# A pinned order for the head of a fused attention and two-layer network kernel, with a score bank pair for each of the first four units and eight products with zeros

## The chip, the cores and the metric

The kernel runs on one core of a Trainium2 chip. The metric is the device time of one execution in microseconds (us); less is better. TensorE (PE in the rows; PEld is its weight load) multiplies, VectorE (DVE) and ScalarE (ACT) work on elements, SyncE (SP) issues the DMAs. Each engine executes its own instructions strictly in the order in which they stand in its queue, and an instruction waits at the head of its queue until what it needs is there.

## The reference, cut to what matters

Sliding-window attention with global tokens gives x (2304 rows of 512), then two feed-forward layers follow, each with 2048 hidden columns. The change touches the attention of the first tokens and the start of the first layer.

```python
s_l = concat([q_l @ k_g.T, where(|i - j| <= 32, q_l @ k_l.T, -1e9)]) / 8
out_l = softmax(s_l) @ concat([v_g, v_l])        # 4 batches, 8 heads, 512 rows, 64 columns
x = out.transpose(0, 2, 1, 3).reshape(2304, 512)
h = x @ w_in
g = maximum(h, 0) + alpha * minimum(h, 0)        # PReLU
x = g @ w_out
h = x @ w2_in
x = (h * clip(h + 3, 0, 6) / 6) @ w2_out
```

## The kernel before

**Attention units.** The local attention is cut into 32 units: one batch, one half of the 512 rows, one pair of heads. A unit loads q and k (`qk_t`) and v (`v_t`), computes 32 small score products (`s_ps`, L208), takes the masked maxima on VectorE (L226, four of them with their read-outs), four exponentials on ScalarE (L230), a sum and a reciprocal on VectorE (L232, L234; operations on 128x4), four transposes of the probabilities on TensorE (`pt_ps`, L241), a copy of them out of PSUM (`pt`, L243, ScalarE), the products with v (`o_ps`, L254) and a scaling on VectorE (`xo`, L260). Units are worked off in pairs, and both units of a pair write their scores into one pair of PSUM banks.

**First layer.** Products in float32 are made of three products of parts: every operand is split into a high part (a rounding copy on ScalarE) and a low part (a subtraction on VectorE). The outputs of four units (one per pair of heads) make 256 rows of x: they are transposed (`xt_ps`, L426) and split into `xt` (L409 high, L410 low). The weights arrive as 64-bit floats and are converted by hand, in halves of 128x512 (`Weights.convert`): ScalarE makes the low words usable (`raw`, L110), VectorE scales the high words (`z`, L113), merges both by two bit operations (L121, L123), and then the half is split (`wt`, L132 high on ScalarE, L133 low on VectorE). Each of the 16 column blocks j has two halves, one for the product into the hidden layer and one for the product out of it. A hidden step s is a group of 12 products (`h_ps`, L459), the PReLU (`t`, L469 on ScalarE and L471 on VectorE) and the split of its result (`g`, L477 high, L478 low); two steps later come the 12 products out of the layer (`y_ps`, L490).

**Block 0.** The first block of 512 rows begins with its first 256 rows, which four units give (units 0 to 3): steps 0 to 3 work on these with columns j = 0 to 3. Units 4 to 7 give the second 256 rows; steps 4 to 7 repeat j = 0 to 3 on them, and from step 8 on the products are 128x512 wide, over both halves. This document calls the `xt` of units 4 to 7 the second half of x.

**What sets the order.** A scheduler orders each engine's queue by its own estimate of times. An instruction passed through `here(...)` (keep_in_program_order) keeps its place in the order of the code relative to the others so marked. Before, the marks stand on the first two steps of a weight conversion and on `c1_sb`; the rest of the head is the scheduler's. `while not ready(blocks[0][:1])` drives the attention generator until units 0 to 3 are done, with a weight half converted at its steps 3, 4 and 5 (`CONVERT`). `bank()` hands out PSUM banks, in the head in turn from two pools of four.

**Head and rest.** Eight products of zeros (`warm_ps`, L87) stand at the very start of TensorE's queue.

## Time and profile before

| what | value |
|---|---|
| time, median of 3 runs | 825.03 us (823.32 to 825.47) |
| time of the profiled execution | 823.27 us |
| its span, first to last instruction | 821.5 us |
| mean granted clock of TensorE over the span | 0.993 of 2.4 GHz |
| busy TensorE / VectorE / ScalarE | 809.2 / 596.6 / 423.3 us |
| TensorE without a gap | from about 50 us to the end stage |

A row of the timeline gives the start of an instruction (or of a run of equal ones), its length, engine, line of the kernel, tile written <- tiles read, shape and count; in brackets the time that the engine sat idle before it and what released it. Rows of equal instructions overlap by some 0.1 us, since the end of one is recorded after the next has begun; the distance from one start to the next is what an instruction costs its queue.

### The profile page before, as it was taken

The page shows a single profiled execution, that of the slowest core. Times are in us where ns is not written, and L with a number is a line of the kernel's source. Part 1 is how long each engine was busy: PE and PEld are TensorE (multiplying, and loading weights), DVE is VectorE, ACT ScalarE, POOL GpSimd, SP SyncE. Part 2 cuts the span into 40 slices and gives each one's busy share as a digit, 9 for nine tenths or more (in the row PEclk, how much of TensorE's full clock was granted, in tenths as well). Part 3 has the DMA queues.
Part 4 walks back from the last instruction along what each step waited for, and adds up shares of the span by engine and source line. Part 5 has one row for each costly group of instructions (what it writes and reads, how often), then busy time and mean ns, then how long its engine had stood idle before and what let it go on. Part 6 is the DMA issues. An engine that isn't in the chain of part 4 may idle for free.

```text
span 821.5 us, 17564 instructions
## 1 busy us (share of the span) xinstructions
PE 809.2 (99%) x6980; PEld 714.1 (87%) x6980; DVE 596.6 (73%) x1247; ACT 423.3 (52%) x886; POOL 0.2 (0%) x4
## 2 busy tenths in 40 slices
PE   7999999999999999999999999999999999999997
PEld 4788888888888887888999988889999888899997
DVE  4998997477888776756878847778867576678443
ACT  5887996445656664544545524434553343333431
POOL 0000000000000000000000000000000000000000
PEclk8899999999999999999999999999999999999999
DMA  9985674347879767788495575576686656655663
GB/s 334 354 276 193 244 251 149 107 175 261 280 252 305 246 236 250 276 282 284 159 335 174 167 257 180 183 225 207 185 268 212 201 186 204 180 181 159 208 182 108
DMA packets 78002, 183.09 MB, mean 223 GB/s; under 512 B 6752, under 2 KB 28512, under 8 KB 77920
## 3 DMA queue, kind: packets, MB, share of 16 engines
q1 hardware_dynamic: 77728, 181.83, 66.9%
q8 instruction: 55, 0.90, 0.4%
q14 instruction: 27, 0.22, 0.1%
q10 hardware_dynamic: 192, 0.13, 0.1%
HBM read 139.47 MB, written 42.47 MB: 221 GB/s over the span
## 4 chain that ended last, share of the span: by engine, by line
PE 93%; DVE 2%; ACT 2%; DMA 1%; SPq 1%; issue 0%; DVEq 0%; ACTq 0%
PE y_ps L490 23%; PE h_ps L459 22%; PE o_ps L904 20%; PE k_ps L816 19%; PE s_ps L208 2%; PE o_ps L254 2%; PE yr_ps L789 1%; PE hr_ps L768 1%; DMA raw<-in_w 1%; PE pt_ps L241 1%; ACT p L230 1%; PE go_ps L391 1%; PE xt_ps L426 1%; PE gs_ps L346 1%; DVE z L121 1%
## 5 line engine op out<-in xcount | busy, mean ns | idle before, releaser
L490 PE MATMUL y_ps<-g,wt 128*128 128x512 f32 (+2 forms) x1008 | 205.4, 353 | 0.2 <-ACT g L477 0.2
L459 PE MATMUL h_ps<-xt,wt 128*128 128x512 f32 (+2 forms) x1008 | 203.2, 352 | 1.9 <-DVE xt L410 1.6
L459 PEld LDWEIGHTS h_ps<-xt,wt 128*128 128x128 f32 x1008 | 169.2, 190 | 24.0 <-DVE xt L410 2.0
L490 PEld LDWEIGHTS y_ps<-g,wt 128*128 128x128 f32 x1008 | 166.7, 189 | 22.2 <-issue 0.8
L904 PE MATMUL o_ps<-ws,gh 128*128 128x256 f32 x896 | 160.9, 283 | 0.1
L816 PE MATMUL k_ps<-bt,ws 128*128 128x512 f32 x672 | 157.2, 390 | 0.0
L816 PEld LDWEIGHTS k_ps<-bt,ws 128*128 128x128 f32 x672 | 124.6, 188 | 24.9
L904 PEld LDWEIGHTS o_ps<-ws,gh 128*128 128x128 f32 x896 | 138.8, 192 | 0.6 <-issue 0.3
L904 PE MATMUL o_ps<-ws,gl 128*128 128x256 f32 x448 | 124.2, 283 | 0.0
L830 DVE TENSOR_TENSOR gl<-far,gh 128x1024 fp32r<-128x1024 f32 x56 | 68.5, 1223 | 42.3 <-ACT gh L829 42.3
L829 ACT CAST gh<-far 128x1024 fp32r<-128x1024 f32 x56 | 58.7, 1048 | 74.4 <-PE o_ps L904 70.6
L904 PEld LDWEIGHTS o_ps<-ws,gl 128*128 128x128 f32 x448 | 84.9, 192 | 0.0
L471 DVE SCALAR_TENSOR_TENSOR t<-t,c_sb,h_ps 128x512 f32<-128x512 f32 (+2 forms) x84 | 53.0, 641 | 30.0 <-ACT t L469 29.6
L750 ACT ACTIVATE t<-far,half_sb 128x512 f32<-128x512 f32 x48 | 34.8, 724 | 77.1 <-DVE far L746 77.1
L469 ACT ACTIVATE t<-h_ps 128x512 f32<-128x512 f32 (+2 forms) x76 | 41.5, 550 | 51.0 <-PE h_ps L459 49.0
L478 DVE TENSOR_TENSOR g<-t,g 128x512 fp32r<-128x512 f32 (+2 forms) x76 | 48.0, 632 | 20.8 <-ACT g L477 18.4
L477 ACT CAST g<-t 128x512 fp32r<-128x512 f32 (+2 forms) x76 | 43.8, 576 | 34.7 <-DVE t L471 33.4
L230 ACT ACTIVATE p<-p,st 128x128 f32<-128x128 f32 x128 | 49.7, 389 | 11.6 <-DVE st L226 11.6
L121 DVE SCALAR_TENSOR_TENSOR z<-z,raw 128x512 uint32<-128x512 uint32 x64 | 43.6, 689 | 9.1 <-ACT z L116 4.6
L110 ACT ACTIVATE raw<-raw,quarter_sb 128x512 uint32<-128x512 uint32 x64 | 49.3, 772 | 1.6 <-DMA raw<-in_w 1.6
L123 DVE SCALAR_TENSOR_TENSOR z<-raw,z 128x512 uint32<-128x512 uint32 x64 | 43.4, 688 | 0.6
L751 DVE SCALAR_TENSOR_TENSOR far<-t,far 128x512 f32<-128x512 f32 x48 | 33.1, 689 | 11.8 <-ACT t L750 11.8
(102 smaller groups left out, 786.5 us busy)
## 6 DMA issues: line engine op xcount, KB each, us to landing
raw<-in_w SPq DMA_DIRECT2D x64, 512.0 KB, 5.4
ws<-wo SPq DMA_DIRECT2D x60, 512.0 KB, 3.8
ws<-wi SPq DMA_DIRECT2D x56, 512.0 KB, 4.4
v_t<-in_vE SPq DMA_DIRECT2D x32, 512.0 KB, 6.9
qk_t<-in_qkE SPq DMA_DIRECT2D x32, 368.0 KB, 5.1
wi<-raw SPq DMA_DIRECT2D x16, 512.0 KB, 3.3
wi<-parts SPq DMA_DIRECT2D x16, 512.0 KB, 4.5
wo<-raw SPq DMA_DIRECT2D x16, 512.0 KB, 2.9
```

What stands on the lines that cost most here:

```text
L110: here(nc.scalar.activation(low, low, AF.Relu, bias=quarter_sb, scale=0.9 * 2.0 ** -29))
L121: nc.vector.scalar_tensor_tensor(out=bits, in0=bits, scalar=3, in1=low, op0=ALU.logical_shift_left, op1=ALU.bitwise_or)
L230: nc.scalar.activation(p[:, n, :], p[:, n, :], AF.Exp, bias=st[:, 1, n:n + 1], scale=-1.0, accum_out=st[:, 2, n:n + 1])
L459: nc.tensor.matmul(ps[:, a:b], lhsT=wts[j][:, 0, wl, 128 * c:128 * c + 128], rhs=xt[c][:, xl, at:at + b - a], start=k == 0, stop=k == 3 * ...
L471: nc.vector.scalar_tensor_tensor(out=t[:, c:d], in0=t[:, c:d], scalar=c1_sb[:, j:j + 1], in1=ps[:, c:d], op0=ALU.mult, op1=ALU.add)
L477: nc.scalar.copy(g[:, 0, a:b], t[:, a:b])
L478: nc.vector.tensor_tensor(out=g[:, 1, a:b], in0=t[:, a:b], in1=g[:, 0, a:b].bitcast(F32), op=ALU.subtract)
L490: nc.tensor.matmul(y[c][:, at:at + b - a], lhsT=wts[j][:, 1, wl, 128 * c:128 * c + 128], rhs=g[:, gl, a:b], start=first, stop=last, skip_g ...
L816: nc.tensor.matmul(bank, lhsT=wt[:, wl, 128 * c:128 * c + 128], rhs=bt[x][:, c, xl, 0:w], start=first and k == 0, stop=k == 5, skip_group_ ...
L829: nc.scalar.copy(hi, src)
L830: nc.vector.tensor_tensor(out=lo, in0=src, in1=hi.bitcast(F32), op=ALU.subtract)
L904: mm = nc.tensor.matmul(bank, lhsT=part[:, jp, 128 * c:128 * c + 128], rhs=wo[:, jp, 256 * wl:256 * wl + 256], start=opens, stop=k == NP / ...
```

## The change

- `keep` pins every instruction of units 0 to 3, of the first half of x and of the first hidden step with its PReLU into the order of the code; it is switched off behind that first step (`pinned["on"] = False`).
- Each of the units 0 to 3 has its own pair of score banks, and its maxima and exponentials are written directly behind its scores.
- The transposed probabilities of units 0 to 2 are copied out of PSUM by VectorE, that of unit 3 by ScalarE as before.
- Units 0 to 3 give their values one by one instead of in pairs; the four transposes and splits of x are written between them.
- The weight conversion `W1.one()` is a generator whose pieces are placed by hand: of the first half between the splits of x, of the second half around the first PReLU. `CONVERT` goes, and at step 0 the two calls ahead of the products fall away.
- Eight products with zeros (4, 2 and 2) are put between the last steps of the head.
- `load(4)` moves ahead of the scores; the loads of v for units 4 and 5 move behind the values of unit 1.

The core of the diff:

```diff
+    def keep(x):
+        return here(x) if pinned["on"] else x
+
+    def idle_products(n):
+        fill = bank("warm_ps")
+        for _ in range(n):
+            keep(nc.tensor.matmul(fill, lhsT=still.to_broadcast([128, 128]), rhs=still.to_broadcast([128, 512]),
+                                  start=True, stop=True))
...
+        def one(self):
...
+            self.begin(k)
+            yield
+            if k + 1 >= SCALED_ON_DVE:
+                self.begin(k + 1)
+            yield from split_w(self.begun.pop(k), self.wt[j], m)
...
+        for u in range(FIRST_UNITS):
+            s = [bank("s0_ps"), bank("s1_ps")]
+            scores(u, s, 0)
+            maxima(u, s, 0)
+            exponentials(u)
+        t = {}
+        for u in range(2):
+            t[u] = transposes(u)
+            sums(u)
+            transposed(u, t[u], nc.vector.tensor_copy)
...
+        t[2] = transposes(2)
+        values(0)
+        sums(2)
+        transposed(2, t[2], nc.vector.tensor_copy)
+        t[3] = transposes(3)
+        sums(3)
+        values(1)
+        yield
...
-    k = 0
-    while not ready(blocks[0][:1]):
-        attention_steps(1)
-        k += 1
-        if k in CONVERT:
-            W1.convert(1)
     xt = x_tiles()
-    x_split(x_transposed(blocks[0][:1]), xt, 0)
+    half = W1.one()
...
+    t1 = turn(1)
+    idle_products(4)
+    high_x(t1, xt[1], 256)
+    next(half)
+    low_x(t0, xt[0], 256)
+    low_x(t1, xt[1], 256)
+    next(half)
+    attention_steps(1)
+    next(half)
+    idle_products(2)
+    t2 = turn(2)
+    high_x(t2, xt[2], 256)
+    attention_steps(1)
+    low_x(t2, xt[2], 256)
+    idle_products(2)
+    t3 = turn(3)
+    high_x(t3, xt[3], 256)
+    low_x(t3, xt[3], 256)
...
+    half = W1.one()
+    next(half)
+    next(half)
...
-                    W1.convert(W1.needed(converted(s)) - W1.next)
-                    W1.convert(min(1, W1.needed(converted(s) + AHEAD) - W1.next))
+                    if s:
+                        W1.convert(W1.needed(converted(s)) - W1.next)
+                    if s:
+                        W1.convert(min(1, W1.needed(converted(s) + AHEAD) - W1.next))
                 parts = active(bi, s)
-                gs[s] = act(0, h_tile(xt, W1.wt, parts), parts)
+                gs[s] = act(h_tile(xt, W1.wt, parts), parts, half)
+                pinned["on"] = False
```

How the queues change, at three places (line numbers are those of each kernel's own file).

TensorE's queue of the changed kernel, from the transposes of the first two units' outputs (`xt_ps`) to the first hidden step (`h_ps`):

```order
L478 MATMUL xt_ps<-consts_sb,xo 128x128 x4
L108 MATMUL warm_ps<-still 128x512 x4
L286 MATMUL o_ps<-v_t,pt 32x64 x16
L108 MATMUL warm_ps<-still 128x512 x2
L478 MATMUL xt_ps<-consts_sb,xo 128x128 x2
L286 MATMUL o_ps<-v_t,pt 32x64 x16
L108 MATMUL warm_ps<-still 128x512 x2
L478 MATMUL xt_ps<-consts_sb,xo 128x128 x2
L511 MATMUL h_ps<-xt,wt 128x256 x12
```

The eight products with zeros (`warm_ps`) stand ahead of the values of unit 2, of the transposes of unit 2 and of those of unit 3; before, no such product stood there.

VectorE's queue before, behind the PReLU of step 1 (`g_531`); `t_582` is the PReLU of step 2:

```order
L478 TENSOR_TENSOR g_531<-t_530,g_531 128x256
L113 TENSOR_SCALAR z_538<-raw_385 128x512
L121 SCALAR_TENSOR_TENSOR z_538<-z_538,raw_385 128x512
L471 SCALAR_TENSOR_TENSOR t_582<-t_582,c1_sb_73,h_ps_569 128x256
L133 TENSOR_TENSOR wt_331<-z_509,wt_331 128x512
L123 SCALAR_TENSOR_TENSOR z_538<-raw_385,z_538 128x512
L226 ISA p_635,st_636<-s0_ps_601,consts_sb_72 128x128
L226 ISA st_636 128x1
```

VectorE's queue of the changed kernel at the same place, behind the PReLU of step 1 (`g_548`); five more rows of weight conversion and then the PReLU of step 2 (`t_599`) follow:

```order
L528 TENSOR_TENSOR g_548<-t_547,g_548 128x256
L143 TENSOR_TENSOR wt_339<-z_443,wt_339 128x512
L122 TENSOR_SCALAR z_453<-raw_407 128x512
L122 TENSOR_SCALAR z_526<-raw_438 128x512
L130 SCALAR_TENSOR_TENSOR z_453<-z_453,raw_407 128x512
L130 SCALAR_TENSOR_TENSOR z_526<-z_526,raw_438 128x512
L132 SCALAR_TENSOR_TENSOR z_453<-raw_407,z_453 128x512
L132 SCALAR_TENSOR_TENSOR z_526<-raw_438,z_526 128x512
L143 TENSOR_TENSOR wt_451<-z_453,wt_451 128x512
L143 TENSOR_TENSOR wt_409<-z_526,wt_409 128x512
L122 TENSOR_SCALAR z_555<-raw_449 128x512
L130 SCALAR_TENSOR_TENSOR z_555<-z_555,raw_449 128x512
```

Before, two operations on weights stand between the PReLUs of the steps 1 and 2; now sixteen do, which finish four weight halves and merge a fifth.

TensorE's queue before, around the transposes (`xt_ps`) of units 4 to 7 and the first products on the second half of x (`h_ps` behind them):

```order
L254 MATMUL o_ps<-v_t,pt 32x64 x32
L426 MATMUL xt_ps<-consts_sb,xo 128x128 x4
L490 MATMUL y_ps<-g,wt 128x256 x12
L426 MATMUL xt_ps<-consts_sb,xo 128x128 x4
L459 MATMUL h_ps<-xt,wt 128x256 x16
L490 MATMUL y_ps<-g,wt 128x256 x4
L459 MATMUL h_ps<-xt,wt 128x256 x6
L241 MATMUL pt_ps<-consts_sb,p 128x128 x4
L459 MATMUL h_ps<-xt,wt 128x256 x2
L241 MATMUL pt_ps<-consts_sb,p 128x128 x4
L490 MATMUL y_ps<-g,wt 128x256 x8
L459 MATMUL h_ps<-xt,wt 128x256 x24
```

The same place in the changed kernel:

```order
L222 MATMUL s_ps<-qk_t 32x128 x32
L286 MATMUL o_ps<-v_t,pt 32x64 x32
L478 MATMUL xt_ps<-consts_sb,xo 128x128 x2
L540 MATMUL y_ps<-g,wt 128x256 x21
L478 MATMUL xt_ps<-consts_sb,xo 128x128 x2
L540 MATMUL y_ps<-g,wt 128x256 x3
L478 MATMUL xt_ps<-consts_sb,xo 128x128 x4
L511 MATMUL h_ps<-xt,wt 128x256 x22
L270 MATMUL pt_ps<-consts_sb,p 128x128 x4
L511 MATMUL h_ps<-xt,wt 128x256 x2
L270 MATMUL pt_ps<-consts_sb,p 128x128 x4
L511 MATMUL h_ps<-xt,wt 128x256 x24
```

The products out of the layer (`y_ps`), of which 12 stood behind the first products on the second half, now all stand ahead of them. From the first 128x512 row of `h_ps` on, which follows in both when one more pair of units has given its scores and values, TensorE's queue is the same row by row to the end.

## Rows read from the trace of the kernel before

**Rows 1.** Windows: busy time of each engine, TensorE's granted clock, DMA.
```profile
30.00:40.00 10.00, 9.13 (x180) 7.24 (x183) 9.40 (x36) 9.43 (x28) 0.00 (x0) 1.00 0.89 300
40.00:50.00 10.00, 8.29 (x164) 6.93 (x156) 9.42 (x39) 9.61 (x34) 0.00 (x0) 1.00 0.90 310
50.00:60.00 10.00, 10.00 (x107) 9.53 (x113) 8.90 (x18) 8.12 (x18) 0.00 (x0) 1.00 0.75 255
```

**Rows 2.** Timeline of TensorE: start, length, instruction, count, idle time before.
```profile
48.74 0.85 PE L459 MATMUL h_ps<-xt,wt 128*128 128x256 f32 x5 [1.25 <-DVE xt L410]
49.89 1.57 PE L459 MATMUL h_ps<-xt,wt 128*128 128x256 f32 x11 [0.30 <-DVE xt L410]
...
53.53 1.19 PE L490 MATMUL y_ps<-g,wt 128*128 128x256 f32 x8
54.56 3.04 PE L459 MATMUL h_ps<-xt,wt 128*128 128x256 f32 x24
...
63.34 2.91 PE L459 MATMUL h_ps<-xt,wt 128*128 128x512 f32 x12
```

**Rows 3.** Timeline of VectorE: start, length, instruction, count.
```profile
21.47 0.42 DVE L113 TENSOR_SCALAR z<-raw 128x512 f32<-128x512 f32 x1
21.80 0.68 DVE L133 TENSOR_TENSOR wt<-z,wt 128x512 fp32r<-128x512 f32 x1
22.40 0.68 DVE L121 SCALAR_TENSOR_TENSOR z<-z,raw 128x512 uint32<-128x512 uint32 x1
...
23.67 0.68 DVE L123 SCALAR_TENSOR_TENSOR z<-raw,z 128x512 uint32<-128x512 uint32 x1
24.27 0.68 DVE L121 SCALAR_TENSOR_TENSOR z<-z,raw 128x512 uint32<-128x512 uint32 x1
24.99 0.69 DVE L123 SCALAR_TENSOR_TENSOR z<-raw,z 128x512 uint32<-128x512 uint32 x1
...
26.20 0.28 DVE L226 CUSTOM_DVE_ANT_0 p<-s_ps,consts_sb 128x128 f32<-128x128 f32 x1
...
26.41 0.29 DVE L226 CUSTOM_DVE_ANT_0 p<-s_ps,consts_sb 128x128 f32<-128x128 f32 x1
...
46.19 0.74 DVE L260 TENSOR_TENSOR xo<-o_ps,rs 128x256 f32<-128x256 f32 x2
46.85 0.40 DVE L478 TENSOR_TENSOR g<-t,g 128x256 fp32r<-128x256 f32 x1
```

**Rows 4.** Timelines of TensorE, VectorE and ScalarE in the first 18 us.
```profile
4.62 1.60 PE L208 MATMUL s_ps<-qk_t 64*32 64x128 f32 x64
...
6.31 0.29 DVE L226 CUSTOM_DVE_ANT_0 p<-s_ps,consts_sb 128x128 f32<-128x128 f32 x1 [5.39 <-PE s_ps L208]
...
13.39 0.39 ACT L230 ACTIVATE p<-p,st 128x128 f32<-128x128 f32 x1
...
17.06 0.43 DVE L113 TENSOR_SCALAR z<-raw 128x512 f32<-128x512 f32 x1 [1.11 <-DMA raw<-in_w]
```

**Rows 5.** Groups by line and form, 0 to 60 us: count, busy, mean ns.
```profile
L110 ACT ACTIVATE raw<-raw,quarter_sb 128x512 uint32<-128x512 uint32 x13 | 9.9, 771 | 1.6 <-DMA raw<-in_w 1.6
...
L254 PE MATMUL o_ps<-v_t,pt 128*32 128x64 f32 x256 | 5.5, 240 | 1.2 <-DVE xo L260 0.8 <-ACT pt L243 0.2
...
L426 PE MATMUL xt_ps<-consts_sb,xo 128*128 128x128 f32 x16 | 3.9, 362 | 1.7 <-DVE xo L260 1.7
...
L234 DVE RECIPROCAL rs<-st 128x4 f32<-128x4 f32 x10 | 1.7, 174 | 0.3
...
L87 PE MATMUL warm_ps<-still 128*128 128x512 f32 x8 | 3.8, 651 | 0.9 <-DVE quarter_sb L499 0.9
```

**Rows 6.** The same groups over the whole span: the one copy on VectorE.
```profile
L1039 DVE COPY ev<-y_ps 128x512 f32<-128x512 f32 x6 | 4.0, 688 | 2.0 <-PE y_ps L490 2.0
```

**Rows 7.** A window and a row of TensorE's timeline at the lower clock.
```profile
17.00:19.00 2.00, 1.05 (x33) 0.81 (x32) 1.94 (x5) 1.83 (x4) 0.00 (x0) 0.50 1.04 416
...
23.22 2.45 PE L459 MATMUL h_ps<-xt,wt 128*128 128x256 f32 x10
```

More of the change, by code (lines that the diff above doesn't have):

```diff
@@ L43 @@
 SCALED_ON_DVE = 8
-CONVERT = (3, 4, 5)
 SPLIT = (0, 70, 70, 30, 43)
@@ L278, in local_units @@
         yield
+        load(4)
         pairs = [(u, u + 1) for u in range(0, n, 2)]
-        scores(*pairs[0])
+        for u in range(FIRST_UNITS):
+            s = [bank("s0_ps"), bank("s1_ps")]
+            scores(u, s, 0)
+            maxima(u, s, 0)
+            exponentials(u)
+        t = {}
+        for u in range(2):
+            t[u] = transposes(u)
+            sums(u)
+            transposed(u, t[u], nc.vector.tensor_copy)
+        keep(nc.vector.tensor_scalar(out=c1_sb, in0=alpha_sb, scalar1=-1.0, scalar2=1.0, op0=ALU.mult, op1=ALU.add))
+        t[2] = transposes(2)
[5 more added lines that the diff above has]
+        values(1)
         yield
-        scores(*pairs[1])
-        here(nc.vector.tensor_scalar(out=c1_sb, in0=alpha_sb, scalar1=-1.0, scalar2=1.0, op0=ALU.mult, op1=ALU.add))
-        load(4)
         load(5)
+        transposed(3, t[3], nc.scalar.copy)
         yield
-        for u in pairs[0]:
-            transposes(u)
-        yield
-        values(*pairs[0])
         load_v(4)
         load_v(5)
-        for u in pairs[1]:
-            transposes(u)
+        values(2)
         yield
-        values(*pairs[1])
+        values(3)
         yield
@@ L300, in local_units @@
                 for u in pairs[j - 1]:
-                    transposes(u)
+                    turned(u)
                 yield
@@ L305, in local_units @@
             if j < len(pairs):
-                scores(*pairs[j])
+                probabilities(*pairs[j])
             if j > 2:
```

175 lines of the change are left out of this document (96 added, 79 removed).

## The prediction

> **What bounds the kernel now.** I read the windows first. From 50 us on TensorE is busy 10 us of 10, and before that it is not [rows 1]; so what the change is worth is how far it moves the moment from which TensorE never waits again. The timeline of TensorE gives that moment: the last two gaps, 1.25 and 0.30 us, end at 48.74 and 49.89, both released by VectorE's low parts of the second half of x (L410), and the first 128x512 product starts at 63.34 [rows 2]. From that product on the order is the same in both kernels, so I call it the joint and forecast its start. The reader should see which engine is late ahead of it: VectorE is busy 9.40 and 9.42 of 10 us from 30 to 50 us [rows 1], and ScalarE as much, but VectorE is the one that releases TensorE. VectorE's timeline gives what each operation costs the queue, from start to start: a scaling of weights 0.33, a bit operation or a low part of weights 0.60, 0.72 where a bit operation follows its own predecessor, a maximum 0.21, a 128x256 operation on x or g 0.33 (the pair at 46.19) [rows 3].
>
> **The change part by part.** *Own score banks.* Before, the first maximum waits until 6.31 for the scores of units 0 and 1, which take from 4.62 to 6.22 [rows 4]; now it needs unit 0's alone, about half: start near 5.4, a gain of 0.9. At least the constants could hold it back; the bounds are 0 and 0.9.
>
> *Copies moved to VectorE.* No row shows this copy on VectorE; the nearest is the copy of a 128x512 result, 0.69 us [rows 6]. Three make 2.1 us on VectorE, and ScalarE is freed to run its 16 exponentials without a break: 5.4 + 0.3 + 16 x 0.39 = 11.9, where the last one ended at 13.78 before [rows 4].
>
> *The pinned chain* from there to the last low part of the first half of x (I call its end A, the point where VectorE turns to the second weight half). Transposes of unit 3 and values of unit 1, 0.2 + 0.7 (5.5 us for the values of 8 units [rows 5]): 12.8. VectorE is through its 16 maxima by about 9.6 and then has eight small operations (0.17 each), three copies and one scaling, 1.4 + 2.1 + 0.3, so it scales unit 1's output at 13.4. Transposes 0.4, high part 0.4, ScalarE's pass over the raw half 0.77 [rows 5]: 15.4. Two bit operations, 0.72 + 0.68: 16.8. Then unit 2's scaling, transposes, unit 3's values, scaling, transposes, a high and a low part, 0.4 + 0.4 + 0.7 + 0.4 + 0.4 + 0.4 + 0.4 = 3.1: A = 19.9. All this is at TensorE's full clock. Before, the granted clock fell to 0.50 in this stretch, that is to the lower level, with TensorE busy about half of a window [rows 7]; at that level the TensorE steps of the chain double and A is 21.3. A cannot be before 17.06, when the second raw half lands [rows 4].
>
> *The zeros.* A product of zeros costs 0.47 (8 in 3.8 us [rows 5]) or at full clock half that. Four stand ahead of unit 2's values, from 14.2 on: they end at 15.1 to 16.1, and the values with 0.7 behind them at 16.8 at the latest, when VectorE is just through its bit operations: hidden. Two and two more stand behind values and cover waits for a scaling; with the cover gone they cost 0.5 each time. What they can give is the clock. The Trainium skill ("TensorE: Matmul & The Clock Gate", section "What's actually happening") says that the clock is throttled by default and that activity releases it; the fall at half-busy TensorE agrees. By that rule the zeros hold the clock and A is 19.9; by the row of before, without them, 21.3. I take 20.2, nearer to the former, because the first four stand just where TensorE ran empty before; before's own counterpart of A is 21.47, so the lead is 1.3 us.
>
> *The queue behind A.* This is the term that decides. Pinning ends at the first PReLU, and the scheduler's order between A and the scaling of units 6 and 7 (whose outputs are the last part of the second half of x) has changed: it now puts weight halves ahead that stood behind. Counted on VectorE's queue: before, 6 scalings, 12 bit operations, 7 low parts, 24 maxima, 10 operations of 128x256, 8 small ones: 2.0 + 7.2 + 4.2 + 5.0 + 3.3 + 1.4 = 23.1 us; the trace took 21.47 to 46.19 = 24.7, so 1.6 us were stalls. Now 7, 20, 10, 24, 10 and 8: 2.3 + 12.0 + 6.0 + 5.0 + 3.3 + 1.4 = 30.0 us. That is 6.9 more, and the lead at A cannot pay for it. The halves are needed later in any case, but there VectorE has time to spare and TensorE does not wait for it.
>
> *Stalls in that queue.* In before's share (1.6 on 23) they come to 2.1. The new order makes more: a scaling, two bit operations, ScalarE's high part and the low part of one half stand directly behind each other, where each waits for the one ahead. I followed the queue from A: 0.4 for the low part of the second half, 1.0 for the PReLU of step 1 behind eight exponentials and a raw pass on ScalarE, 0.8 and 0.4 for the two halves that are converted alone, 0.4 in smaller waits, and 1.3 for bit operations and scalings that follow their own predecessor: 4.3. Bounds 0 and 4.3; I take 3.2.
>
> *Behind it on TensorE.* Before, the joint comes 17.1 us after the scaling at 46.19. Now 12 products out of the layer less stand in that stretch (8 take 1.03, so 12 take 1.5) and the waits of 1.55 fall in with VectorE's: scaling 0.7, transposes 0.7 (four, of 16 in 3.9 us at either clock [rows 5]), 24 products on the second half and 8 transposes 4.0 (from 49.89 to 54.56 without 1.5 for products out, with the five products of 48.74), and 54.56 to 63.34 = 8.8 [rows 2]: 14.2.
>
> *DMA.* The loads of v for units 4 and 5 pass the fourth raw half on SP's queue, and it arrives later by two transfers of 512 KB, some 3 us at the 300 to 400 GB/s of the windows [rows 1, 7]. VectorE needs it only some 9 us behind A, near 29 us: hidden.
>
> **Sum.** Joint = A + queue + stalls + TensorE = 20.2 + 30.0 + 3.2 + 14.2 = 67.6, against 63.3: 4.3 us later, and nothing behind it gives that back, since TensorE has no gap there. The profiled execution took 823.27, 1.8 above its span, and the median of the runs shown is 825.03; so 827.6 on the one footing and 829.3 on the other. I forecast 828.5, slower.
>
> **Rivals.** *The stalls vanish.* With A = 19.9 and no stall the joint is at 64.1, 0.8 later: 824 to 826, no change that a measurement of this kernel tells (about 0.3%, 2.5 us). For it speaks that before ran its queue with little stall; against it, the chains of one half standing alone. Up to stalls of 1.6 it ends here.
>
> *The lead is kept (the other side).* If VectorE's queue is not what the second half waits for, everything behind the first hidden step comes earlier by the lead of 1.3 us and the 1.5 us of products out that have moved forward: joint at 60.5, 820.5 to 822.2. It decides where the units' own chain of scores, exponentials and transposes, and not VectorE's place in line, releases the last scaling. Against it: VectorE at 9.4 of 10, and even without any stall the queue alone gives 64.1.
>
> *TensorE falls to the lower clock once more.* With VectorE 3 to 5 us later at the second half, TensorE waits longer there. In before it ran its first 2.45 us of solid products at the lower level after a half-idle stretch, 10 products instead of about 20 [rows 7]; that again costs 1.2 us: 829.7. The Trainium skill (same page, section "Why this matters for your kernels") warns of idle gaps between bursts of matmuls; between 30 and 50 us of before the gaps cost nothing, as the granted clock stayed at 1.00 [rows 1].
>
> *The zeros hold up the head.* If TensorE stays at the lower clock in spite of them, A is 21.3 and 1 us comes from the zeros themselves: joint 69.7, 829.7 to 831.4.
>
> **How the numbers follow.** Forecast (stalls between 2 and 4.3, clock either way) 0.48; lower clock once more 0.09; zeros hold up 0.09; stalls vanish 0.25; lead kept 0.09. Slower by over 0.3% takes the first three, 0.66, less 0.01 that fall short: 0.65; within 0.3% 0.26; faster 0.09. The range has to reach from the no-stall case, on the profile's footing 824.1 less a microsecond for an A as early as 18.9, to the zeros' case with all stalls, 829.7 + 1.1 and the median's offset: 823.0 to 832.0. The forecast's own range is 826.5 to 831.
>
> **What the profile of the changed kernel will show.** First maximum near 5.4 and last exponential ended near 12; last low part of the first half of x before 20.5, the first hidden products behind it and ScalarE's first PReLU operation near 21. VectorE solid from there with short waits for ScalarE's high parts; scaling of units 6 and 7 at 52 to 54.5 instead of 46.19; TensorE's last gap before some 56; the joint at 66 to 69. If the scaling stands at 50 or earlier, the count of the queue or its prices are wrong; if it stands late and the joint is early all the same, TensorE's 14.2 is. If the granted clock shows 0.50 around 17 us, the zeros did not hold it. A joint later than 63.3 with an unchanged time would mean that TensorE made up for it behind, which I take for impossible.

## The result and the profile after

The changed kernel takes 829.61 us (median of 6 runs, 829.09 to 830.93) against 825.23 us for the kernel before (median of 6, 823.32 to 826.36): a ratio of 1.0059, 95% interval 1.0045 to 1.0072. It is slower by more than the 0.3% that such a measurement tells. The profiled execution took 830.57 us, near the top of its runs, where that of before was the fastest of its own (823.27); so the two traces lie 7.3 us apart and the medians 4.4.

The timeline of TensorE after, from the zeros to the first 128x512 product (the joint), answers to [rows 2]:

```profile
14.64 1.14 PE L108 MATMUL warm_ps<-still 128*128 128x512 f32 x4 [0.27 <-PE xt_ps L478]
16.35 0.65 PE L286 MATMUL o_ps<-v_t,pt 128*32 128x64 f32 x32 [0.57 <-DMA v_t<-in_vE]
...
19.54 1.67 PE L511 MATMUL h_ps<-xt,wt 128*128 128x256 f32 x12
21.13 0.67 PE L222 MATMUL s_ps<-qk_t 64*32 64x128 f32 x32
23.19 0.42 PE L222 MATMUL s_ps<-qk_t 64*32 64x128 f32 x6 [1.39 <-DMA qk_t<-in_qkE]
...
30.68 2.93 PE L540 MATMUL y_ps<-g,wt 128*128 128x256 f32 x12 [1.61 <-ACT wt L142]
34.53 0.58 PE L511 MATMUL h_ps<-xt,wt 128*128 128x256 f32 x1 [0.93 <-ACT wt L142]
...
49.69 1.51 PE L222 MATMUL s_ps<-qk_t 64*32 64x128 f32 x48 [1.47 <-DVE t L523]
51.14 1.93 PE L286 MATMUL o_ps<-v_t,pt 128*32 128x64 f32 x64
...
67.43 1.10 PE L286 MATMUL o_ps<-v_t,pt 128*32 128x64 f32 x64
...
69.99 2.91 PE L511 MATMUL h_ps<-xt,wt 128*128 128x512 f32 x12
```

The joint stands at 69.99 instead of 63.34, 6.65 us later. Read the brackets from the top: the head waits for a load of v and the second q/k load of a pair, and from 30 us on TensorE waits for what VectorE and ScalarE make (wt, t), in longer waits than before. The last of them ends at 49.69. The timeline of VectorE after, answering to [rows 3] and [rows 4]:

```profile
5.82 0.29 DVE L240 CUSTOM_DVE_ANT_0 p<-s_ps,consts_sb 128x128 f32<-128x128 f32 x1 [4.90 <-PE s_ps L222]
...
10.42 0.66 DVE L275 COPY pt<-pt_ps 128x512 f32<-128x512 f32 x1
...
20.22 0.43 DVE L458 TENSOR_TENSOR xt<-xt_ps,xt 128x256 fp32r<-128x256 f32 x1 [0.60 <-ACT xt L455]
20.57 0.42 DVE L122 TENSOR_SCALAR z<-raw 128x512 f32<-128x512 f32 x1
...
24.58 0.29 DVE L240 CUSTOM_DVE_ANT_0 p<-s_ps,consts_sb 128x128 f32<-128x128 f32 x1 [0.65 <-PE s_ps L222]
...
30.14 0.43 DVE L528 TENSOR_TENSOR g<-t,g 128x256 fp32r<-128x256 f32 x1 [1.03 <-ACT g L527]
...
31.93 1.29 DVE L130 SCALAR_TENSOR_TENSOR z<-z,raw 128x512 uint32<-128x512 uint32 x2
33.14 1.29 DVE L132 SCALAR_TENSOR_TENSOR z<-raw,z 128x512 uint32<-128x512 uint32 x2
34.51 1.29 DVE L143 TENSOR_TENSOR wt<-z,wt 128x512 fp32r<-128x512 f32 x2
...
38.28 0.69 DVE L143 TENSOR_TENSOR wt<-z,wt 128x512 fp32r<-128x512 f32 x1 [0.69 <-ACT wt L142]
...
48.59 0.66 DVE L143 TENSOR_TENSOR wt<-z,wt 128x512 fp32r<-128x512 f32 x1
49.16 0.47 DVE L523 SCALAR_TENSOR_TENSOR t<-t,c_sb,h_ps 128x256 f32<-128x256 f32 x1
...
55.58 0.75 DVE L292 TENSOR_TENSOR xo<-o_ps,rs 128x256 f32<-128x256 f32 x2
...
57.41 1.06 DVE L458 TENSOR_TENSOR xt<-xt_ps,xt 128x256 fp32r<-128x256 f32 x3
```

The head works: the last low part of the first half of x starts at 20.22 and ends at 20.57 (before, the last one started at 23.00). Later come weight halves, at first two at a time, from 31 to 40 us with nothing else between them, and the scaling of units 6 and 7 stands at 55.58 where it stood at 46.19. The windows after: the stretch from the last low part of the first half to that of the second, then those that answer to [rows 1], and three of the head for later:

```profile
20.22:57.41 37.19, 29.00 (x440) 23.29 (x439) 33.14 (x111) 28.83 (x86) 0.00 (x0) 0.82 0.85 304
30.00:40.00 10.00, 8.40 (x100) 6.89 (x104) 8.90 (x16) 5.39 (x10) 0.00 (x0) 0.50 0.67 235
40.00:50.00 10.00, 6.72 (x129) 5.33 (x129) 9.57 (x36) 9.20 (x29) 0.00 (x0) 1.00 0.83 280
50.00:60.00 10.00, 10.00 (x165) 9.26 (x154) 7.96 (x33) 7.18 (x26) 0.00 (x0) 0.83 0.89 312
...
13.00:16.00 3.00, 2.33 (x36) 1.31 (x24) 1.88 (x8) 1.90 (x4) 0.00 (x0) 1.00 1.02 411
16.00:19.00 3.00, 2.51 (x69) 1.79 (x70) 2.51 (x6) 1.00 (x2) 0.00 (x0) 1.00 1.02 415
19.00:22.00 3.00, 2.80 (x48) 2.08 (x47) 2.26 (x6) 1.44 (x3) 0.00 (x0) 1.00 1.04 405
```

In the first line VectorE is busy 33.14 of 37.19 us. The window of the same stretch in before has 25.96 of 27.95:

```profile
23.00:50.95 27.95, 25.10 (x397) 20.66 (x390) 25.96 (x101) 24.73 (x81) 0.00 (x0) 0.96 0.93 331
```

That gives an account in four terms, used for every kernel below: **A'**, the start of the last low part of the first half of x; **work**, VectorE's busy time from there to X, the start of the last group of low parts of the second half; **idle**, the rest of that stretch; **behind**, from X to the joint. From before to after A' moves by -2.78, work by +7.18, idle by +2.06 (1.99 to 4.05), behind by +0.19 (12.39 to 12.58): +6.65. The sum is exact by construction; what can be wrong is a forecast of a term. And in both traces the time is the joint and 760 to 761 us (759.93 and 760.58): nothing behind the joint gives anything back.

The account runs along VectorE, and X is a landmark on it, not the end of TensorE's last wait. That wait ends at 49.89 before [rows 2] and at 49.69 after: 1.47 us for the PReLU of step 3 (`t`, L523 at 49.16), which stands on VectorE behind low parts of weights. From there TensorE has 20.30 us of work without a gap up to the joint; before it had 13.45. VectorE is nearly full there too (0.20 us idle from 49.69 to the scaling at 55.58), so the trace after does not tell which of the two engines sets the joint behind that wait. On TensorE's own line the joint is its busy time (the second number of a window) and its idle time; before, after, and after from the last wait on:

```profile
0.00:63.34 63.34, 55.30 (x937) 43.99 (x938) 49.83 (x194) 49.75 (x152) 0.20 (x4) 0.92 0.89 318
...
0.00:69.99 69.99, 58.06 (x944) 45.65 (x945) 53.07 (x198) 49.32 (x149) 0.20 (x4) 0.90 0.80 287
49.69:69.99 20.30, 20.25 (x352) 18.52 (x353) 15.68 (x59) 16.68 (x49) 0.00 (x0) 0.92 0.64 215
```

Of the 6.65 us, 3.89 are idle time (8.04 to 11.93) and 2.76 busy time, of which the eight zeros are 2.54. So the changed kernel is later because TensorE waits more for the others, and hardly because its own products take longer.

### The profile page after: what moved, and what is told of

It is laid out like the page before. It is cut to its first block, busy times and chain, and to the rows that moved or that the text cites. A ratio compares the mean times of both kernels' runs of the same rounds, so it can differ in the third digit from the quotient of the medians.

```text
span 828.8 us, 17586 instructions
## 1 busy us (share of the span) xinstructions
PE 812.3 (98%) x6988; PEld 715.9 (86%) x6988; DVE 599.7 (72%) x1250; ACT 422.4 (51%) x883; POOL 0.2 (0%) x4
## 4 chain that ended last, share of the span: by engine, by line
PE 94%; ACT 2%; DMA 1%; DVE 1%; issue 0%; ACTq 0%
PE y_ps L540 23%; PE h_ps L511 22%; PE o_ps L952 19%; PE k_ps L864 18%; PE s_ps L222 2%; PE o_ps L286 2%; PE yr_ps L837 1%; PE hr_ps L816 1%; DMA qk_t<-in_qkE 1%; PE pt_ps L270 1%; ACT p L248 1%; PE xt_ps L478 1%; PE gs_ps L392 1%; PE go_ps L437 1%; PE warm_ps L86 0%; PE gpt_ps L419 0%
## 5 line engine op out<-in xcount | busy, mean ns | idle before, releaser
L540 PEld LDWEIGHTS y_ps<-g,wt 128*128 128x128 f32 x1008 | 168.5, 191 | 23.4 <-ACT wt L142 1.8
L523 DVE SCALAR_TENSOR_TENSOR t<-t,c_sb,h_ps 128x512 f32<-128x512 f32 (+2 forms) x84 | 53.1, 643 | 34.0 <-ACT t L521 33.7
```

Of the source, the lines that this page charges most:

```text
L523: keep(nc.vector.scalar_tensor_tensor(out=t[:, c:d], in0=t[:, c:d], scalar=c1_sb[:, j:j + 1], in1=ps[:, c:d], op0=ALU.mult, op1=ALU.add))
L540: nc.tensor.matmul(y[c][:, at:at + b - a], lhsT=wts[j][:, 1, wl, 128 * c:128 * c + 128], rhs=g[:, gl, a:b], start=first, stop=last, skip_g ...
```

## The experiments

Two theories ahead of the runs. **Order**: what the scheduler puts on VectorE (and TensorE) between the first half of x and the scaling of units 6 and 7 makes the loss, and the head is a gain. **Rivals**: the zeros hold up the head; the pinned head or the copies in it do; it is something that an edit does by itself, whatever the order becomes. A "count" is a number of VectorE operations in the order, each at the price of its row as in the prediction. All were timed in five rounds, and each ratio is to the kernel before on the same chip beside it (medians 824.6 to 825.2 us).

**Attention steps earlier.** Only the table that gives out the units' steps changes:

```diff
-STEPS = [[2] * 4 + [1] * 16, [1] * 16, [1]*11+[2]*3+[1]*2, [2] * 8, [0] * 16]
+STEPS = [[4, 2, 2, 0] + [1] * 16, [1] * 16, [1]*11+[2]*3+[1]*2, [2] * 8, [0] * 16]
```

> The changed kernel with the eight attention steps behind the first hidden steps given out as 4, 2, 2, 0 and no longer 2, 2, 2, 2 (one number in a table); the pinned head, the banks and the zeros stay. The order then puts 36.4 us of VectorE work by the row prices ahead of the last scaling of units 6 and 7 (the changed kernel 41.2, the kernel before 33.8, all counted from the first operation), and 8 low parts of weights ahead of the last low part of x (11 and 8). Theory queue (VectorE's line of weight halves ahead of units 6 and 7 makes the loss): that scaling at 49 to 51 (changed 55.6, before 46.2), the joint, the first 128x512 product, at 64.5 to 67 (changed 70.0, before 63.3; 36 products out of the layer stand behind the second half again, 1.5 us more than in the changed kernel), time 1.001 to 1.003 of the kernel before. Rival zeros (the zeros hold up the head) and rival head (the pinned head itself comes too late): the joint stays near 70 and the time at 1.006, since neither is touched.

Measured: 826.04 us, 1.0017 (1.0007 to 1.0027). Its window from A' to X:

```profile
20.07:51.89 31.82, 25.26 (x432) 19.93 (x431) 29.62 (x108) 27.66 (x84) 0.00 (x0) 0.93 0.94 333
```

The joint stands at 65.31, inside what the theory of the order gave, and the scaling at 48.46, half a microsecond ahead of it. Work is 29.62 for 33.14 and idle 2.20 for 4.05. So some 3.5 of the 4.4 us come back with head, banks, copies and zeros untouched; neither rival on the head can do that. On TensorE's own line, however, only 1.57 of the 4.68 us by which the joint is earlier are idle time; 3.11 are busy time on the same products, at a granted clock of 0.93 for 0.82 in the windows from A' to X. The order behind the head makes the loss; this run does not separate the line on VectorE from the clock at which TensorE runs behind its waits.

**Fewer halves ahead.** The line is shortened in another way:

```diff
-                        W1.convert(min(1, W1.needed(converted(s) + AHEAD) - W1.next))
+                        W1.convert(min(1, W1.needed(converted(s) + (AHEAD if s >= DELAY else 1)) - W1.next))
...
-                    W1.convert(W1.needed(converted(s) + AHEAD) - W1.next)
+                    W1.convert(W1.needed(converted(s) + (AHEAD if s >= DELAY else 1)) - W1.next)
```

> The changed kernel with one half of weights wanted ahead and no longer two, in the first four hidden steps alone; all else stays. By the order 36.0 us of VectorE work stand ahead of the last scaling of units 6 and 7 and 9 low parts of weights ahead of the last low part of x. Theory queue: that scaling at 49 to 51, the joint at 65 to 67, time 1.001 to 1.004 of the kernel before; it is another way than the table of steps to shorten the same line, so both must bring the joint forward by like amounts. Rivals zeros and head: joint near 70, 1.006.

Measured: 833.96 us, 1.0110 (1.0097 to 1.0123): a miss, 4 us slower than the changed kernel where 2 to 4 us faster was expected. Work did fall as counted, to 29.64. TensorE's timeline shows where it went:

```profile
31.47 3.10 PE L540 MATMUL y_ps<-g,wt 128*128 128x256 f32 x12 [3.40 <-ACT wt L142]
34.37 0.41 PE L511 MATMUL h_ps<-xt,wt 128*128 128x256 f32 x1
34.71 1.06 PE L222 MATMUL s_ps<-qk_t 64*32 64x128 f32 x18
...
44.62 0.58 PE L511 MATMUL h_ps<-xt,wt 128*128 128x256 f32 x1 [3.43 <-ACT wt L142]
```

Two groups of products now wait for a half that is converted just ahead of them (3.40 and 3.43 us), and the scores (L222) of the next units stand behind them in TensorE's queue. VectorE then has nothing to do: idle is 10.60 us. The count alone is not a law; a shorter line helps only if the units' own chain does not end up behind a wait.

**No zeros.** The eight products feed nothing:

```diff
         fill = bank("warm_ps")
-        for _ in range(n):
+        for _ in range(0):
```

> The changed kernel without its eight products with zeros (they feed nothing); the VectorE order is the same, 41.2 and 11. Theory queue: the end of the first half of x, now 20.6, and the scaling of units 6 and 7 move by less than 1.5 us and the time stays at 1.005 to 1.007. Rival zeros-hold-up: the first half comes 1 us or more earlier, joint 69 or less, 1.004. The other way round, if the zeros hold the clock: granted clock near 0.5 somewhere from 13 to 22 us (1.00 in the changed kernel), first half of x at 21.5 to 22, joint near 71, 1.007 to 1.008.

Measured: 828.67 us, 1.0052 (1.0039 to 1.0065), an interval that overlaps that of the changed kernel: neither a cost nor a gain of the zeros can be told. The windows of the head without zeros, to be read beside the last three of the changed kernel above:

```profile
13.00:16.00 3.00, 1.80 (x64) 1.15 (x52) 2.41 (x8) 1.78 (x4) 0.00 (x0) 1.00 1.01 414
16.00:19.00 3.00, 1.04 (x35) 0.71 (x35) 2.52 (x6) 0.99 (x2) 0.00 (x0) 1.00 1.03 415
19.00:22.00 3.00, 3.00 (x29) 2.78 (x37) 2.26 (x5) 1.23 (x3) 0.00 (x0) 0.59 1.03 399
```

With the zeros the granted clock reads 1.00 from 19 to 22 us and without them 0.59, but the head is nearly through by then: A' is 19.86 without them and 20.22 with them. The later part that I gave for the lower clock (A at 21.5 to 22) did not come. The joint of this execution is 1.9 earlier (68.08), 1.5 of it in idle time (2.53 for 4.05), where the load that TensorE waited 1.39 us for in the changed kernel's trace was not waited for. On TensorE's line the difference is busy time, the zeros' own (58.06 to 56.03, with idle time 11.93 and 12.05), so a cost of the zeros of up to the 0.9 us between the medians is not ruled out.

**Banks alone.** The kernel before, with one part of the change:

```diff
-        scores(*pairs[0])
-        yield
-        scores(*pairs[1])
+        scores(0)
+        scores(1)
+        yield
+        scores(2)
+        scores(3)
```

> The kernel before with one part of the change alone: the scores of units 0 to 3 get banks of their own, one after the other; nothing is pinned, no zeros, no copy moved. The order's count is 36.5 us of VectorE work ahead of the last scaling of units 6 and 7 and 10 low parts of weights ahead of the last low part of x (before 33.8 and 8), 24 products out of the layer behind the second half as in the changed kernel. Theory queue: first maximum near 5.8 and yet the scaling of units 6 and 7 later than 46.2, at 47 to 50, joint at 63.5 to 66, time 1.000 to 1.003 of the kernel before. Rival pin (the pinned head or the zeros make the loss, the banks are a gain): joint at 62.5 or earlier, 0.997 to 0.999.

Measured: 827.44 us, 1.0033 (1.0020 to 1.0046), joint 67.83 in a profiled execution of 828.08; a little more than the theory gave, and opposite in sign to the rival. VectorE's timeline:

```profile
5.82 0.29 DVE L226 CUSTOM_DVE_ANT_0 p<-s_ps,consts_sb 128x128 f32<-128x128 f32 x1 [4.90 <-PE s_ps L208]
...
17.34 0.43 DVE L113 TENSOR_SCALAR z<-raw 128x512 f32<-128x512 f32 x1 [1.88 <-DMA raw<-in_w]
...
23.28 0.41 DVE L412 TENSOR_TENSOR xt<-xt_ps,xt 128x256 fp32r<-128x256 f32 x1
52.27 0.75 DVE L260 TENSOR_TENSOR xo<-o_ps,rs 128x256 f32<-128x256 f32 x2
```

The first maximum comes as early as in the changed kernel, but that is lost in a longer wait for a raw weight half (1.88 us, 1.11 before [rows 4]) and A' is no earlier than before. Behind it, work is 28.98 for 25.96 and idle 4.01 for 1.99. So the banks alone, with nothing pinned, bring about half of the loss, and the lead in the head comes from the rest of the change. That the longer line on VectorE makes this loss is not shown, though. TensorE's windows up to the joint and from its last listed wait (0.83 us for a weight half, up to 33.04):

```profile
0.00:67.83 67.83, 59.18 (x937) 46.20 (x937) 50.28 (x195) 50.04 (x152) 0.20 (x4) 0.90 0.83 297
33.04:67.83 34.79, 34.62 (x553) 29.88 (x553) 30.72 (x105) 29.60 (x84) 0.00 (x0) 0.90 0.72 237
33.04:40.00 6.96, 6.96 (x84) 5.49 (x88) 6.10 (x13) 4.40 (x10) 0.00 (x0) 0.51 0.42 139
```

TensorE is idle 8.65 us up to the joint, hardly more than before (8.04); what is longer is its busy time on the same products, 59.18 for 55.30, with the granted clock at 0.51 from 33 to 40 us. The eight runs point the same way: the three with a mean granted clock over the whole span of 0.993 or more took 825.9 to 826.4 us, the five below it 827.3 to 830.2, where the kernel before has a median of 825.17. By these few runs (an estimate) about half of the loss of the banks goes with the clock.

**Copies on ScalarE.** The changed kernel with its three copies moved back:

```diff
-            transposed(u, t[u], nc.vector.tensor_copy)
+            transposed(u, t[u], nc.scalar.copy)
...
-        transposed(2, t[2], nc.vector.tensor_copy)
+        transposed(2, t[2], nc.scalar.copy)
```

> The changed kernel with the three copies of transposed probabilities back on ScalarE (0.58 us each from start to start on VectorE in the changed kernel); all else stays. The order's count ahead of the scaling of units 6 and 7 is 39.5 us for 41.2, the 1.7 us of the copies, and the line of weight halves is as long as in the changed kernel (11). Theory order (what stands on VectorE and TensorE between the first half of x and the scaling of units 6 and 7 makes the loss): the copies lie ahead of the first half of x, which waits for other things; the joint between 69 and 70.5, time 1.005 to 1.007. Rival copies (VectorE has too much to do in the head): the first half of x 1 us earlier or more, joint at 68.5 or less, 1.004 or less.

Measured: 832.59 us, 1.0094 (1.0081 to 1.0107): both theories missed, the copies on VectorE are a gain. One row of TensorE's timeline shows the first part of it, the first values waiting for a copy that now stands on ScalarE behind all the exponentials:

```profile
12.61 0.65 PE L286 MATMUL o_ps<-v_t,pt 128*32 128x64 f32 x32 [1.67 <-ACT pt L275]
```

A' is 0.72 later and the joint 1.14 (71.13), which is less than the 3.0 us between the medians (829.61 and 832.59); the profiled execution was the fastest of these runs (831.12). The rest of that difference stays open.

**Values first.** Steps as in the first experiment, and for units 6 and 7 the values ahead of the next scores:

```diff
+            if j == 4:
+                values(*pairs[j - 1])
             if j < len(pairs):
                 probabilities(*pairs[j])
-            if j > 2:
+            if j > 2 and j != 4:
                 values(*pairs[j - 1])
```

> The kernel with attention steps given out earlier (4, 2, 2, 0), and besides the value products of units 6 and 7 written ahead of the scores of units 8 and 9 (elsewhere the scores stay ahead). The count ahead of the scaling of units 6 and 7 falls from 36.4 to 32.8, as 8 maxima and some weights now stand behind it; that ahead of the last low part of x stays at 40.7 (40.8). Theory order in the sense that the wait of the scores of units 8 and 9 for a bank and for their step is on the path: scaling 2 to 4 us earlier than with the steps alone (48.5 there), joint at 62 to 64.5, 0.997 to 1.000. Rival line of low parts (what counts is all VectorE work ahead of the last low part of the second half of x, and that is the same): scaling earlier, but joint at 64.5 to 66 and time at 1.001 to 1.003.

Measured: 825.69 us, 1.0020 (1.0009 to 1.0030), joint 66.97. The scaling stands at 46.18, 2.3 us earlier than with the steps alone, and the time is the same. Work up to X is 29.57 for 29.62. So an earlier scaling alone, the point at which the prediction closed its sum, gains nothing. TensorE's last wait in this trace is for a low part of the second half:

```profile
52.14 4.40 PE L513 MATMUL h_ps<-xt,wt 128*128 128x256 f32 x22 [1.02 <-DVE xt L460]
```

The joint of this execution is 1.66 later than with the steps alone, past the 66 of the rival, and idle time (4.08 for 2.20) makes it so.

**Pin longer.** The order is kept as written through three PReLU steps:

```diff
-                pinned["on"] = False
+                pinned["on"] = s < 2
```

> The changed kernel with the order kept as it is written through the first three PReLU steps and no longer up to the first alone; all else stays. Count ahead of the scaling of units 6 and 7 36.4 us (41.2), 9 low parts of weights ahead of the last low part of x (11), 36 products out of the layer behind the second half (24). Theory order: scaling 49 to 53, joint 65 to 68, time 1.001 to 1.004. If the count alone does not matter, as in the kernel with fewer halves wanted ahead (36.0, yet joint at 73.6), it can come out later than the changed kernel, 70 or more: the weights of a step then stand directly ahead of its products, and TensorE waits for them with the units' scores behind it.

Measured: 834.05 us, 1.0115 (1.0102 to 1.0128), joint 73.34, as late as the last sentence of the expectation allowed. Work 30.66, idle 8.89; TensorE waits at 27.34 for a weight half (1.27 us) and, longest, at 32.10 for exponentials (2.82). The scores for these are done by 23.1, but in the kept order their maxima stand on VectorE behind three weight halves:

```profile
31.16 0.28 DVE L240 CUSTOM_DVE_ANT_0 p<-s_ps,consts_sb 128x128 f32<-128x128 f32 x1
```

It is the second kernel in which a smaller count comes with a later joint.

**Control: steps in the kernel before.** The same line of the table as in the first experiment, in the kernel before.

> Control: the kernel before with the attention steps given out as 4, 2, 2, 0 and nothing else. Count ahead of the scaling of units 6 and 7 34.1 us (before 33.8), 8 low parts of weights ahead (8). Theory order: nothing to gain, since its order is already so: joint 62.5 to 64.5, 0.998 to 1.002. Rival (the table of steps is a gain of its own that has nothing to do with the line the change makes): as much as in the changed kernel, 3 us or more, 0.996 or less.

Measured: 827.07 us, 1.0031 (1.0017 to 1.0044). The rival (a gain of its own) is out; the theory's "nothing" is missed by 0.1%. Work is 26.19, as in before (25.96), but A' is 0.96 later and 15.30 us lie behind X for 12.39, and around X TensorE waits three times (1.03, 0.64 and 0.55 us) for low and high parts of x and a weight half; the granted clock there is 0.89, before 1.00. A part of the lateness of A' is this execution's: its first maximum came at 7.01 for 6.31, although VectorE's and TensorE's order up to there is that of before. With its count unchanged this control is as slow as the banks alone (1.0033, with a count of 36.5), so among edits of the kernel before the counts do not sort the times.

**Fewer scalings on VectorE.** `SCALED_ON_DVE` says how many halves VectorE scales. Three kernels: 8 to 4 on top of the earlier steps, 8 to 2 in the changed kernel, and 8 to 2 in the kernel before, where the order answers the other way. For the first:

```diff
-SCALED_ON_DVE = 8
+SCALED_ON_DVE = 4
```

> The kernel with attention steps given out earlier (4, 2, 2, 0), and besides only the first four weight halves scaled on VectorE and no longer eight; the later ones are scaled on ScalarE (0.65 us each there). The order's count of VectorE work ahead of the last low part of x is 38.3 us (with the steps alone 40.8, changed kernel 43.8, before 38.9). Theory line of low parts (the joint is the end of the first half of x, plus VectorE's work and idle time up to the last low part of the second half, plus 12 to 13.4 us): 20.1 + (29.6 - 2.5) + 2.2 to 4 + 13.4 = joint at 62.8 to 64.6, time 0.998 to 1.001 of the kernel before. Rival ScalarE (it takes VectorE's place as what is late): joint at 65.5 to 67, 1.002 to 1.004.

> The changed kernel with one number changed: only the first two weight halves are scaled on VectorE, the later six of the eight on ScalarE. With it the order falls out otherwise too: 8 low parts of weights ahead of the last low part of x (11), count 37.6 us (43.8), 36 products out of the layer behind the second half (24). Theory line of low parts: 20.2 + (33.1 - 6.2) + 2 to 5 idle + 12.6 to 13.4 = joint at 62 to 66, time 0.997 to 1.002. Rival ScalarE: six scalings of 0.65 us fall on ScalarE, which is busy 9.2 of 10 us from 40 to 50 in the changed kernel: idle time on VectorE grows by about what is saved, joint at 68 to 70, 1.004 to 1.006.

> Control: the kernel before with the same number changed (two halves scaled on VectorE). Here the count ahead of the last low part of x does not fall but rises, 38.9 to 40.1, with 11 low parts of weights for 8. Theory line of low parts: 23.0 + (26.0 + 1.2) + 2 to 4 + 12.4 = joint at 64.5 to 66.6, time 1.001 to 1.004. Rival (scaling on ScalarE is a gain or a loss of its own, whatever the order does): the same sign and size as in the changed kernel with this number.

Measured: 825.21 us, 1.0005 (0.9994 to 1.0015), joint 62.65, for the first; 825.23 us, 1.0003 (0.9992 to 1.0013), joint 64.86, for the second; 827.77 us, 1.0033 (1.0022 to 1.0045), joint 67.16, for the control. VectorE's work from A' to X is 26.97 (expected 27.1), 26.34 (26.9) and 27.85 (27.2). One number thus takes the loss out of the changed kernel and puts 3 us into the one before, both with the sign that the counts gave; the rival gave the same sign twice. The size of the control is not shown to be the count's: of the 3.82 us by which its joint is later, 1.89 are work and 1.45 a later A', and the control above, whose count had not changed, lost as much (1.0031). In both changed kernels the order also puts 12 products out of the layer back behind the second half, so the line on VectorE and the order on TensorE were never moved apart. ScalarE did not become the bound, though it is busy 10.00 of 10 us from 30 to 50 in the second. The control's joint is 0.6 later than the range because its head was late (A' 24.45).

**Second half one step earlier.** `DELAY` 4 to 3, steps 3, 3, 2, in the changed kernel:

```diff
-DELAY = 4
-STEPS = [[2] * 4 + [1] * 16, [1] * 16, [1]*11+[2]*3+[1]*2, [2] * 8, [0] * 16]
+DELAY = 3
+STEPS = [[3, 3, 2] + [1] * 16, [1] * 16, [1]*11+[2]*3+[1]*2, [2] * 8, [0] * 16]
```

> The changed kernel with the second half of x wanted after three hidden steps and no longer four, the eight attention steps given out as 3, 3, 2. Count ahead of the last low part of x 36.4 us, 6 low parts of weights. Some 24 products of 128x256 fewer stand on TensorE ahead of that part, 3.0 us, which then lie behind it. Theory line of low parts: last low part at 20.2 + (33.1 - 7.4) + 2 to 5 = 48 to 51 (before 50.95), so TensorE's last wait ends as early as before or earlier, but with 3.0 us less done: time 823 to 827 where before takes 824.6 to 825.2, 0.998 to 1.003. Rival TensorE order (scores stand behind products that wait for weights, as where the order was kept longer): last low part at 54 or later, 1.005 or more.

Measured: 824.27 us, 0.9990 (0.9981 to 0.9999): the best of all, 5.3 us below the changed kernel, yet against the kernel before still inside the 0.3%. Its windows:

```profile
20.62:49.21 28.59, 23.97 (x411) 18.90 (x410) 25.33 (x100) 23.43 (x76) 0.00 (x0) 0.82 0.93 339
25.00:28.00 3.00, 2.58 (x9) 1.69 (x10) 3.00 (x18) 2.85 (x16) 0.00 (x0) 0.59 1.03 401
28.00:31.00 3.00, 3.00 (x21) 2.34 (x20) 2.34 (x8) 2.16 (x6) 0.00 (x0) 0.50 1.03 404
31.00:34.00 3.00, 3.00 (x54) 2.00 (x57) 1.42 (x4) 2.43 (x5) 0.00 (x0) 0.50 0.60 211
```

Work is 25.33 (expected 25.7) and X at 49.21, inside the 48 to 51. No kernel here beats the one before by more than the measurement tells.

The account of the profiled executions, in us (in the last kernel the joint stands one hidden step earlier in the program, with 24 products fewer ahead of it); the column on TensorE is its idle time from 0 to the joint:

| kernel | A' | work | idle | behind | joint | TensorE idle | profiled time | median |
|---|---|---|---|---|---|---|---|---|
| before | 23.00 | 25.96 | 1.99 | 12.39 | 63.34 | 8.04 | 823.27 | 825.23 |
| changed | 20.22 | 33.14 | 4.05 | 12.58 | 69.99 | 11.93 | 830.57 | 829.61 |
| steps early | 20.07 | 29.62 | 2.20 | 13.42 | 65.31 | 10.36 | 825.68 | 826.04 |
| fewer ahead | 20.00 | 29.64 | 10.60 | 13.31 | 73.55 | 14.18 | 833.90 | 833.96 |
| no zeros | 19.86 | 33.11 | 2.53 | 12.58 | 68.08 | 12.05 | 828.63 | 828.67 |
| banks alone | 23.28 | 28.98 | 4.01 | 11.56 | 67.83 | 8.65 | 828.08 | 827.44 |
| copies on ScalarE | 20.94 | 33.13 | 4.44 | 12.62 | 71.13 | 15.28 | 831.12 | 832.59 |
| values first | 19.49 | 29.57 | 4.08 | 13.83 | 66.97 | 10.05 | 826.34 | 825.69 |
| pin longer | 20.73 | 30.66 | 8.89 | 13.06 | 73.34 | 13.80 | 836.04 | 834.05 |
| before, steps early | 23.96 | 26.19 | 2.50 | 15.30 | 67.95 | 10.49 | 828.22 | 827.07 |
| steps early, 4 scalings | 19.69 | 26.97 | 2.31 | 13.68 | 62.65 | 9.67 | 823.31 | 825.21 |
| 2 scalings | 19.88 | 26.34 | 4.98 | 13.66 | 64.86 | 9.44 | 825.23 | 825.23 |
| before, 2 scalings | 24.45 | 27.85 | 2.31 | 12.55 | 67.16 | 11.62 | 827.50 | 827.77 |
| delay 3 | 20.62 | 25.33 | 3.26 | 13.83 | 63.04 | 8.30 | 824.70 | 824.27 |

The joint carries the time: the profiled time less the joint is 759.4 to 761.7 in all but one of the fourteen, over joints from 62.65 to 73.55. The exception is the longer pin (762.7), where TensorE waits 1.3 us in three places far behind the joint. Joint less TensorE's idle time is its busy time. With the 2.5 us of the zeros taken off it is 55.3 before and 55.5 in the changed kernel, but over the kernels with the same products it reaches from 50.4 (steps early, 4 scalings) to 59.2 (banks alone), and the granted clock differs between them; a joint is therefore not a matter of VectorE's line alone.

## Why the prediction was right, and where its steps were off

- **Direction and mechanism** were right: a shorter head, a longer line on VectorE behind it, TensorE late at the second half, nothing given back. The forecast of 828.5 is 1.1 below the median, inside its own 826.5 to 831.
- **Own banks**: the first maximum stands at 5.82, a gain of 0.5 where 0.9 was taken, since the 32 scores of unit 0 alone take 1.11 us and not half of 1.60; the last exponential ended at 12.33 for "near 12".
- **A** was put at 20.2 and is 20.57. Its working on the clock was wrong: I weighed 19.9 with the zeros against 21.3 without them, and without them it is no later (19.86 against 20.22 at the start of that low part). Without them the granted clock fell only from 19 us on, and the last TensorE step of this chain, two transposes, had started at 18.98. The lead was put at 1.3 from a wrong row: 21.47 is a scaling of weights, and the last low part of the first half stands at 23.00 in before; like for like the lead is 2.78. The sum does not use it. (Two sums in the working are off by little: the 15.4 is reached only with the scaling's own 0.4, which is not listed, and the upper end of the range adds up to 832.6, not 832.0.)
- **The queue behind A** was counted at 30.0. VectorE was busy 31.6 us from 20.22 to 55.58, of which 0.35 is the low part itself: the prices were 1.3 short, where the prediction had put 1.3 for operations behind their own predecessor among the stalls. Queue and stalls together were 33.2 and took 35.0. The surplus over before, which decides, is about right: 6.9 counted, 8.0 measured over the same stretches (31.27 us of work from 20.57 to 55.58, 23.31 from 21.47 to 46.19). The step that closed the sum at the scaling was loose: TensorE's last wait ended at 49.69 already, for a PReLU behind weight halves and not for the second half of x, and with the values first an earlier scaling gained nothing. That it cost nothing here is partly luck: TensorE, full from 49.69 on, reaches the first product on the second half (56.98) within a microsecond of the end of the scaling (56.33).
- **Stalls** were taken at 3.2; VectorE was idle 35.36 - 31.62 = 3.7 us. Of the list, 1.0 for the PReLU of step 1 (1.03) and 0.8 and 0.4 for the halves alone (0.69 and 0.29) came as followed. Not in the list is a wait of 0.65 for the scores of unit 5. A (0.4) and the queue with its stalls (1.8) make 2.2 of the 2.4 us by which the joint is later than 67.6.
- **Behind it on TensorE**: 14.2 forecast, 55.58 to 69.99 = 14.4.
- **DMA**: the raw half is hidden, as forecast, but a load that I did not follow is not. The q/k of unit 5 is issued at 11.98 and lands at 23.15, as the chain of waits after shows, while the DMA share is 1.01 to 1.04, and TensorE waits 1.39 us for it:

```profile
11.98 11.17 DMA qk_t<-in_qkE
```

- **Rivals.** The stalls did not vanish. The lead is not kept: A' is 2.8 earlier and the joint 6.65 later. The zeros do not hold up the head. TensorE did fall to the lower clock once more: 0.50 from 30 to 40 us, and again behind its last wait, where 64 products with v took 1.93 us (at 51.14) for 1.10 at the full clock (67.43). That is 0.8 us, near the 1.2 that was priced; whether the joint pays it is not shown, since VectorE is full up to the scaling. With delay 3 the clock stood at 0.50 from 28 to 34 in the fastest kernel of all. The Trainium skill ("TensorE: Matmul & The Clock Gate", section "Why this matters for your kernels") warns of idle gaps between bursts of matmuls. In the trace after, the clock fell between 28 and 31 us, when TensorE was busy 1.28 of 3 us and no single wait was above 1.61; that the changed kernel as a whole lost time by it is not seen (55.5 us busy for 55.3).
- **What stays open**: why separate banks make the scheduler bring weight halves forward (that they do is shown by banks alone); the full size of the copies' gain; why three unlike edits of the kernel before all cost 0.3%; and how the loss divides between VectorE's line, TensorE's order and the granted clock. Shown is that it lies behind the head: five kernels that keep the head (A' from 19.5 to 20.6) and change what stands behind it are 3.6 to 5.3 us faster than the changed kernel by their medians.

## What to carry to other kernels

When an order is pinned up to some point and left to a scheduler behind it, cost the order behind that point first: here 2.8 us won ahead of it were followed by 9.4 us lost behind it, and one number in a table took most of the net loss back. Count the late engine's work up to the last operation that the bound engine waits for, and find that operation in the rows; and look who stands behind each wait, since twice a shorter line was slower: once scores stood behind products that waited for their weights, once maxima stood behind weight halves. Before blaming a longer line, split the bound engine's time into busy and idle: with the banks alone it was the busy time that had grown. An early gain counts only up to the next thing that is late: the banks' half microsecond went into a wait for a weight load.

## What the runs showed of the hardware that was not expected

- Without the zeros the granted clock stayed at 1.00 from 16 to 19 us with TensorE busy 1.04 of 3 us, and read 0.59 from 19 to 22, when it was busy all the time; in the kernel before it was 0.50 around 17 us [rows 7].
- The same products kept TensorE busy 55.30 us up to the joint in the kernel before and 59.18 with the banks alone, where the granted clock was 0.51 from 33 to 40 us.
- A q/k load of 368 KB took 11.2 us from issue to landing in the crowded head, and the same load made TensorE wait 0.7 to 1.5 us in seven of the ten kernels with the pinned head.
- A copy of 128x512 on VectorE took 0.66 us, close to the row it was priced by [rows 6], and a product of zeros 0.28 to 0.35 us at the full clock.
